# A linear-attention network on one core: every phi by two operations on ScalarE and one on VectorE, block sums moved behind the last keys, denominators at another pace

## The chip, the cores and the metric

The kernel runs on one core of one Trainium2 chip. The metric is the device time of one execution in microseconds (us). PE is TensorE's matmuls, PEld its weight loads, DVE is VectorE, ACT is ScalarE, POOL is GpSimd, SP the engine that issues most DMAs.

## The reference, cut to what matters

Four layers: linear attention (A), gated ReGLU (B), A, B, each on a layer norm and added back. x is 2048 x 1024, with 32 heads of 32.

```python
phi = lambda t: jnp.where(t > 0, t + 1, jnp.exp(t)) + 1e-6
pq, pk = phi(q), phi(k)
kv  = jnp.einsum("bhsd,bhse->bhde", pk, v)
z   = jnp.einsum("bhsd->bhd", pk)
num = jnp.einsum("bhqd,bhde->bhqe", pq, kv)
den = jnp.einsum("bhqd,bhd->bhq", pq, z)[..., None] + 1e-6
o = num / den          # then reshaped and multiplied by wo
```

Per attention there are 64 phis of 128 x 512 (32 of keys, 32 of queries).

## The kernel before

PE projects 128 x 512 blocks of keys and queries into PSUM banks (four "a" banks, and in the first three quarters two spare ones). A bank is free again when the last instruction of its phi has read it. In quarters 0 to 2 keys and queries alternate; the last quarter does its keys alone, then the products of keys and inputs over block sums, then its queries, between which stand four "folds" (kv times wo) with four copies each.

```python
def phi(self, ps, out, kind):
    nc = self.nc
    e = self.temp(dtype=BF16 if kind == "v" else F32)
    if kind == "v":
        nc.scalar.activation(out=e, in_=ps, func=ACT.Exp)                            # L375
    else:
        nc.scalar.activation(out=e, in_=ps, func=ACT.Relu, scale=-1.0)               # L377
        nc.scalar.activation(out=e, in_=e, func=ACT.Exp, scale=-1.0)                 # L378
        nc.scalar.activation(out=e, in_=e, func=ACT.Identity, bias=self.eps6[:, 0:1])# L379
    def join():
        if kind == "v":
            nc.vector.tensor_scalar(out=e, in0=e, scalar1=1.0, scalar2=1e-6,         # L383
                                    op0=ALU.min, op1=ALU.add)
        nc.vector.scalar_tensor_tensor(out=out, in0=ps, scalar=0.0, in1=e,           # L385
                                       op0=ALU.max, op1=ALU.add)
    # ... (in the first quarter join is put off by three steps)

# keys: always "v". Queries: "s", but "v" in the last quarter (of the second attention: half of it)
self.phi(project(f"q{c}", sc, j), pq[:, c * NW:(c + 1) * NW],
         "s" if sc < self.NQ - 1 or (l and j < 2) else "v")

# m_products, first attention: 64 block sums on VectorE (L485), four per step of PE
for n, (f, i) in enumerate(jobs):
    later.at(1 + n // 4, lambda f=f, i=i: f(i))
# ...
later.at(2 if l else 8, lambda: z_chain(0))

def z_chain(i):                     # denominators, one row of 128 after another
    z_mult(*divmod(i, QT))          # POOL multiplies (L595), DVE sums (L600) and inverts,
    if i < 10:                      # POOL scales the queries (L607)
        later.at(2, lambda: z_chain(i + 1))

def fold_wo(n):                     # ... 16 matmuls of 32x32 weights into four banks, then
    for i in range(R):              # R = 4
        dst = T[g // 4][:, g % 4, n2 * NW:(n2 + 1) * NW]
        nc.scalar.activation(out=dst, in_=ps[i], func=ACT.Copy)                      # L632
```

`later.at(n, f)` puts f into the program n ticks further on; a tick is one unit of PE's work. Vector instructions of the last quarter's queries are issued in program order; elsewhere a scheduler orders them when the kernel is built.

## Time and profile before

| | before |
|---|---|
| time | 1485.1 us, median of 3 (1484.46 to 1485.91) |
| profiled execution | span 1481.5 us, 1483.35 us as timed |
| busy PE, DVE, ACT, POOL | 1464.6, 880.9, 525.3, 285.2 us |
| matmuls | 6975, of which 6692 are of full size and 512 wide (not counting 11 at the start) |

### The profile page before, as it was taken

The page shows a single profiled execution, that of the slowest core. Times are in us where ns is not written, and L with a number is a line of the kernel's source. Part 1 is how long each engine was busy: PE and PEld are TensorE (multiplying, and loading weights), DVE is VectorE, ACT ScalarE, POOL GpSimd, SP SyncE. Part 2 cuts the span into 40 slices and gives each one's busy share as a digit, 9 for nine tenths or more (in the row PEclk, how much of TensorE's full clock was granted, in tenths as well). Part 3 has the DMA queues.
Part 4 walks back from the last instruction along what each step waited for, and adds up shares of the span by engine and source line. Part 5 has one row for each costly group of instructions (what it writes and reads, how often), then busy time and mean ns, then how long its engine had stood idle before and what let it go on. Part 6 is the DMA issues. An engine that isn't in the chain of part 4 may idle for free.

```text
span 1481.5 us, 18698 instructions
## 1 busy us (share of the span) xinstructions
PE 1464.6 (99%) x6975; PEld 664.5 (45%) x6975; DVE 880.9 (59%) x1551; ACT 525.3 (35%) x943; POOL 285.2 (19%) x190
## 2 busy tenths in 40 slices
PE   9989999999999999999999999999999999999999
PEld 4434444444444444444444444444444444444444
DVE  8996798666594543447368856874445434434632
ACT  6742413333340233341057525343333203333300
POOL 1442860111100011110023566401111000111000
PEclk9999999999999999999999999999999999999999
DMA  9930679565458963445943018994444698444461
GB/s 282 243 114 29 171 163 244 179 222 187 160 165 210 350 202 115 144 132 190 305 103 72 1 29 233 269 294 142 139 146 137 179 248 268 143 142 147 149 209 43
DMA packets 318363, 255.51 MB, mean 172 GB/s; under 512 B 105792, under 2 KB 291392, under 8 KB 317376
## 3 DMA queue, kind: packets, MB, share of 16 engines
q1 hardware_dynamic: 308304, 234.00, 54.5%
q10 hardware_dynamic: 9968, 20.32, 3.7%
q8 instruction: 54, 0.88, 0.3%
q14 instruction: 37, 0.30, 0.1%
HBM read 195.04 MB, written 34.60 MB: 155 GB/s over the span
## 4 chain that ended last, share of the span: by engine, by line
PE 88%; DVE 3%; POOL 1%; DMA 0%; issue 0%; SPq 0%; ACT 0%; DVEq 0%
PE yg L830 10%; PE yu L830 10%; PE dy L914 10%; PE ps L435 7%; PE ps L638 7%; PE dv L914 7%; PE dx L914 7%; PE xu L830 6%; PE xg L830 6%; PE vg L830 3%; PE vu L830 3%; PE zu L830 3%; PE zg L830 3%; PE my L517 2%; PE mx L517 2%; PE mv L517 1%
## 5 line engine op out<-in xcount | busy, mean ns | idle before, releaser
L830 PEld LDWEIGHTS <-w 128*128 128x128 f16 (+1 forms) x3136 | 306.5, 98 | 371.1 <-DVE w L764 0.9
L435 PE MATMUL ps<-w,xnT 128*128 128x512 bf16 x1024 | 224.5, 379 | 5.3 <-DVE slab L385 2.6
L868 POOL TENSOR_TENSOR h<-m5u,m5g 128x512 f16<-128x512 f32 x56 | 71.2, 1271 | 809.6 <-DVE m5u L864 787.8
L914 PEld LDWEIGHTS <-h 128*128 128x128 f16 x1120 | 109.6, 98 | 132.1
L861 DVE TENSOR_TENSOR zg<-yg,m5g 128x512 f32<-128x512 f32 x56 | 39.1, 699 | 197.5 <-PE yg L830 197.5
L435 PEld LDWEIGHTS <-xnT 128*128 128x128 bf16 x1024 | 99.4, 98 | 126.3 <-issue 8.8
L638 PE MATMUL ps<-T,pqT 128*128 128x512 bf16 x512 | 111.5, 379 | 4.5 <-DVE pq L385 4.4
L830 PE MATMUL xu<-xnT,w 128*128 128x512 f16 x448 | 115.3, 379 | 0.0
L830 PE MATMUL xg<-xnT,w 128*128 128x512 f16 x448 | 115.1, 379 | 0.0
L830 PE MATMUL yu<-s,w 128*128 128x512 f16 x448 | 115.0, 379 | 0.0
L830 PE MATMUL yg<-s,w 128*128 128x512 f16 x448 | 115.0, 379 | 0.0
L838 ACT ACTIVATE m5g<-m5g 128x512 f32<-128x512 f32 x56 | 35.2, 629 | 199.4 <-DVE m5g L864 199.4
L914 PE MATMUL dy<-w,h 128*128 128x512 f16 x448 | 98.0, 379 | 0.0
L914 PE MATMUL dx<-w,h 128*128 128x512 bf16 x448 | 97.3, 379 | 0.0
L595 POOL TENSOR_TENSOR kvc<-pq,kvc 128x1024 f32<-128x1024 bf16 x32 | 70.1, 2191 | 68.3 <-DVE den L600 48.9
L638 PEld LDWEIGHTS <-pqT 128*128 128x128 bf16 x512 | 50.0, 98 | 65.3 <-issue 5.7
L161 ACT ACTIVATE rstd<-mv,eps 128x1 f32<-128x1 f32 x64 | 18.1, 290 | 167.7 <-DVE mv L159 167.5
L154 DVE BATCH_NORM_STATS2 stats<-x 128x6 f32<-128x512 f32 (+1 forms) x120 | 76.5, 671 | 1.0 <-DMA x<-in_A_x_dram 0.8
L454 POOL TENSOR_TENSOR kvc<-kvc,slab 128x512 f32<-128x512 f32 x46 | 60.7, 1324 | 80.1 <-DVE slab L385 77.7
L841 DVE TENSOR_TENSOR h<-yu,r 128x512 f16<-128x512 f32 x56 | 38.7, 691 | 56.2 <-PE yu L830 56.2
L864 DVE TENSOR_TENSOR m5u<-yu,m5u 128x512 f32<-128x512 f32 x56 | 38.7, 691 | 54.6 <-PE yu L830 54.6
L914 PEld LDWEIGHTS <-e 128*128 128x128 f16 x448 | 43.8, 98 | 52.9
(126 smaller groups left out, 1985.2 us busy)
## 6 DMA issues: line engine op xcount, KB each, us to landing
w<-in_B_W_gate_dram SPq DMA_DIRECT2D x56, 512.0 KB, 6.0
w<-in_B_W_up_dram SPq DMA_DIRECT2D x56, 512.0 KB, 4.8
w<-td SPq DMA_DIRECT2D x32, 896.0 KB, 4.7
w<-in_B_W_down_dram SPq DMA_DIRECT2D x24, 896.0 KB, 5.6
w<-tg SPq DMA_DIRECT2D x42, 512.0 KB, 7.0
w<-tu SPq DMA_DIRECT2D x42, 512.0 KB, 6.1
w<-in_A_wqkv_dram SPq DMA_DIRECT2D x10, 1024.0 KB, 8.1
away<-x SPq DMA_DIRECT2D x16, 512.0 KB, 4.4
```

The lines of the kernel that those rows point to most:

```text
L154: self.nc.vector.bn_stats(out=stats[:, c, :], in_=src[:, c * fmax:(c + 1) * fmax])
L435: nc.tensor.matmul(by_row(ps), lhsT=self.xnT[l, l_q][:, kt, j * P:(j + 1) * P], rhs=w[:, kt, :].rearrange("p (b i d) -> p i b d", i=R, d=H ...
L454: nc.gpsimd.tensor_tensor(out=ksum[:, cols], in0=ksum[:, cols], in1=pk, op=ALU.add)
L517: nc.tensor.matmul(banks[j], lhsT=A(i)[:, j * P:(j + 1) * P], rhs=B(i), start=start and i == 0, stop=i == NS - 1, skip_group_check=True)
L595: nc.gpsimd.tensor_tensor(out=prod, in0=pq_of[sc, j], in1=zrow, op=ALU.mult)
L638: nc.tensor.matmul(ps, lhsT=pqT[sc][:, g, j * P:(j + 1) * P], rhs=T[g // 4][:, g % 4, n2 * NW:(n2 + 1) * NW], start=(g == 0), stop=(g == G ...
L830: nc.tensor.matmul(ps, lhsT=W[w][m][:, k, :], rhs=A[m][:, k, :], start=start and k == 0, stop=k == 3, skip_group_check=True)
L841: self.last_put = nc.vector.tensor_tensor(out=h[:, b, :], in0=ps, in1=R.pop(b), op=ALU.mult)
L861: nc.vector.tensor_tensor(out=Z[w], in0=Y[w], in1=V[w], op=ALU.add)
L864: nc.vector.tensor_tensor(out=V[w], in0=Y[w], in1=V[w], op=ALU.add)
L868: nc.gpsimd.tensor_tensor(out=h[:, 3, :], in0=V["u"], in1=V["g"], op=ALU.mult)
L914: nc.tensor.matmul(banks[j], lhsT=A(k)[:, j * P:(j + 1) * P], rhs=w[:, i, :], start=start and k == 0, stop=k == self.U - 1, skip_group_che ...
```

## The change

Its intent is to take VectorE work out of the way of PE. Each phi becomes exp(1e-6 - relu(-x)) on ACT in two operations and one VectorE instruction, max(x, 1e-6) plus that. The block sums of the first attention are issued behind the last phi of keys. The chain of denominators starts two steps earlier in the first attention and advances by 2 and 3 steps in turn instead of 2.

```diff
-    def phi(self, ps, out, kind):
+    def phi(self, ps, out):
...
-        e = self.temp(dtype=BF16 if kind == "v" else F32)
-        if kind == "v":
-            nc.scalar.activation(out=e, in_=ps, func=ACT.Exp)
-        else:
-            nc.scalar.activation(out=e, in_=ps, func=ACT.Relu, scale=-1.0)
-            nc.scalar.activation(out=e, in_=e, func=ACT.Exp, scale=-1.0)
-            nc.scalar.activation(out=e, in_=e, func=ACT.Identity, bias=self.eps6[:, 0:1])
+        e = self.temp()
+        nc.scalar.activation(out=e, in_=ps, func=ACT.Relu, scale=-1.0)
+        nc.scalar.activation(out=e, in_=e, func=ACT.Exp, scale=-1.0, bias=self.eps6[:, 0:1])
 
         def join():
-            if kind == "v":
-                nc.vector.tensor_scalar(out=e, in0=e, scalar1=1.0, scalar2=1e-6, op0=ALU.min,
-                                        op1=ALU.add)
-            nc.vector.scalar_tensor_tensor(out=out, in0=ps, scalar=0.0, in1=e,
-                                           op0=ALU.max, op1=ALU.add)
+            self.last_phi = nc.vector.scalar_tensor_tensor(out=out, in0=ps, scalar=1e-6, in1=e,
+                                                           op0=ALU.max, op1=ALU.add)
... (callers lose the kind)
+            last_k = self.last_phi
...
-                    later.at(1 + n // 4, lambda f=f, i=i: f(i))
+                    later.at(1 + n // 4, lambda f=f, i=i: self.behind(last_k, f, (i,)))
...
-            later.at(2 if l else 8, lambda: z_chain(0))
+            later.at(2 if l else 6, lambda: z_chain(0))
...
-                later.at(2, lambda: z_chain(i + 1))
+                later.at(2 + i % 2, lambda: z_chain(i + 1))
```

More of the change, by code (lines that the diff above doesn't have):

```diff
@@ L442, in k_unit @@
             pk = self.pk_home(l, t)
-            self.phi(project(f"k{c}", q, j, between), pk[:, c * NW:(c + 1) * NW], "v")
+            self.phi(project(f"k{c}", q, j, between), pk[:, c * NW:(c + 1) * NW])
             later.at(1 + (10 if self.phi_lag else 0), lambda: k_sum(t, slice(c * NW, (c + 1) * NW)))
@@ L582, in q_unit @@
             pq = pq_of[sc, j]
-            self.phi(project(f"q{c}", sc, j), pq[:, c * NW:(c + 1) * NW],
-                     "s" if sc < self.NQ - 1 or (l and j < 2) else "v")
+            self.phi(project(f"q{c}", sc, j), pq[:, c * NW:(c + 1) * NW])
             if c == H - 1 and lag is not None:
```

## The prediction

> **What bounds the kernel now.** I read four views: the page's busy times, who waited for whom with TensorE (PE) as the waiter, busy time by stretch, and the timeline of the worst stretch. The page first (busy us, share of the span, instructions):
>
> ```profile
> PE 1464.6 (99%) x6975; PEld 664.5 (45%) x6975; DVE 880.9 (59%) x1551; ACT 525.3 (35%) x943; POOL 285.2 (19%) x190
> ```
>
> PE is busy for 1464.6 of 1481.5 us, so all that a change on other engines can win is the remaining 16.9 us (1.1%), unless it removes matmuls, which this one doesn't. Is "busy" full speed? The chain of waits shows 112 matmuls of the down projection in 24.17 us, 0.216 us each; my count from the groups is 6692 matmuls 512 wide, 1445 us of the 1464.6. There is no hidden slack, and the granted clock is 1.0 in every stretch. Next, PE's waits (engine, line, releaser: us, times, longest):
>
> ```profile
> PE ps L638 <- DVE pq L385: 4.4, 2, 2.4
> PE ps L435 <- DVE slab L385: 2.6, 3, 1.2
> PE ps L435 <- DVE pq L385: 2.5, 3, 1.2
> PE mx L517 <- DVE slab L385: 1.8, 3, 0.9
> PE idle L246 <- DVE e L243: 1.3, 1, 1.3
> ```
>
> All but the start-up wait have one releaser: L385, the VectorE (DVE) instruction that ends a phi and gives its PSUM bank back. The four come to 11.3 us. Busy time by stretch says when (us, then PE, PEld, DVE, ACT, POOL busy, clock, DMA share, GB/s):
>
> ```profile
> 80.00:117.70 37.70, 31.42 (x141) 13.51 (x140) 36.95 (x61) 14.49 (x24) 18.45 (x13) 1.00 0.38 140
> ...
> 165.00:192.00 27.00, 21.93 (x167) 9.64 (x166) 24.72 (x32) 12.50 (x24) 19.74 (x10) 1.00 0.75 197
> 745.00:850.00 105.00, 105.00 (x488) 47.55 (x487) 87.97 (x157) 64.99 (x113) 39.49 (x31) 1.00 0.27 61
> 850.00:915.00 65.00, 64.91 (x389) 30.97 (x388) 41.18 (x71) 28.11 (x51) 49.65 (x25) 1.00 0.41 100
> ```
>
> PE loses 37.70 - 31.42 = 6.28 us where the first attention's last keys are made, and 27 - 21.93 = 5.07 us where its last queries are. Both times DVE is nearly full (98% and 92%). The second attention (the last two rows) loses 0.09 us. So only the first attention can pay.
>
> Why is DVE full there? The timeline of the last queries, DVE then POOL (GpSimd; in brackets, idle time before and its releaser):
>
> ```profile
> 170.13 1.83 DVE L383 TENSOR_SCALAR e<-e 128x512 bf16<-128x512 bf16 x1
> 172.06 0.69 DVE L385 SCALAR_TENSOR_TENSOR pq<-ps,e 128x512 bf16<-128x512 f32 x1
> 172.67 1.20 DVE L383 TENSOR_SCALAR e<-e 128x512 bf16<-128x512 bf16 x1
> 173.98 0.69 DVE L385 SCALAR_TENSOR_TENSOR pq<-ps,e 128x512 bf16<-128x512 f32 x1
> ```
>
> ```profile
> 169.69 2.12 POOL L595 TENSOR_TENSOR kvc<-pq,kvc 128x1024 f32<-128x1024 bf16 x1 [0.82 <-DVE den L600]
> 171.77 1.96 POOL L607 TENSOR_TENSOR pq<-pq,den 128x1024 bf16<-128x1024 bf16 x1
> ```
>
> L383, the min-and-add that the change deletes, takes 1.83 and 1.20 us and ends just when a POOL instruction ends (171.8, 173.8). Over the whole run:
>
> ```profile
> L383 DVE TENSOR_SCALAR e<-e x76: 241/282/1830, 14.1 to 915.7; 128x512 bf16<-128x512 bf16 x76
> ```
>
> Its median is 282 ns, its maximum 1830, its total 41.4 us (545 ns mean): it is cheap alone and dear beside POOL.
>
> **What the Trainium skill says.** "SBUF — State Buffer", section Who interferes with whom: VectorE and GpSimd share a port pair under an exclusive lock; tensor_scalar can enter a two-port mode and is then blocked for a whole GpSimd instruction; with two SBUF inputs it collides with GpSimd's reads; with at most one SBUF input outside those modes it does not. The trace agrees: L383 (one 16-bit SBUF source) reaches 1830 ns, the block sums L485 (two SBUF inputs) are 0.41 or 1.38 us, and L385 (PSUM and one SBUF input) stays at 0.69 beside the same POOL instructions. "ScalarE: Activation LUTs", section What ACT_TABLE_LOAD costs: a [128,1] pointer operand adds about 93 ns to an ACTIVATE, and ACTIVATEs back to back overlap by about as much. The trace agrees: 630 ns without (L378), 721 with (L379), yet both start 0.63 to 0.66 us apart.
>
> **The change, part by part.**
>
> 1. *VectorE.* 76 of 128 phis ran one ACT and two DVE operations ("v"), 52 three ACT and one DVE ("s"). All 76 L383 go: -41.4 us of DVE, 8.49 of it in 80-117.7, 11.54 in 165-192 (8 instructions), 13.6 in the second attention, where DVE was not in the way.
> 2. *ScalarE (ACT).* "v" goes from 588 ns to 592 + 721: 76 x 0.725 = +55 us. "s" loses an operation but its Exp gains the pointer: 52 x (592 + 721 - 592 - 630 - 721) = -32.8 us. Sum +22 us, 525 to about 548. While keys and queries alternate, the pitch per pair is 0.6 + 1.92 = 2.5 before and 2 x 1.27 = 2.5 after, against 3.46 us of PE for the two. Keys alone: 1.27 per 1.73. Neither binds.
> 3. *Block sums.* The 64 L485 of the first attention may no longer stand among the phis; the rebuilt order shows none ahead of the last key's phi. 18 of them, 11.57 us, leave the stretch 80-117.7. DVE there keeps about 37 - 8.5 - 11.6 = 17 us of work for 31 us of PE, even with all of L785, and PE's 6.28 us go. Are the sums now late? The third block product needs 16 of them, some 14 us after the last key phi; 16 x 0.41 is 6.6 us, 10 with POOL collisions. In the kernel before, DVE then idled 11.23 us. They fit.
> 4. *Last queries.* A period of two queries and a fold: DVE 1.83 + 0.69 + 1.20 + 0.69 + 1.74 (one denominator: 1.21 + 0.18 + 0.35) = 6.15 us, the period seen (170.13 to 176.32). PE needs 2 x 1.73 + 0.43 = 3.9. After: 1.38 + 1.74 = 3.1. PE binds again, and 5.07 us go.
> 5. *Given back.* ACT in that period: four fold copies at 0.48 pitch (1.93) and two phis (2.54) are 4.5 us against 3.9. Four periods leave ACT some 1.7 us behind, and a fold's banks wait for the copies of the fold before. The second attention before had almost this load (four "s" at 1.92, four "v") and lost nearly nothing, but one fold there stretched from 0.43 to 0.70. I choose 0.5 us for each attention: +1.0.
> 6. *Denominators' pace.* 2.5 ticks a row instead of 2 (4.3 against 3.5 us), where a POOL pair takes 4.0: DVE waits less at its head (L600 waited 15.3 us for POOL). PE's own order is unchanged line by line, and the output projections need the late rows long after. Nothing for PE in itself; worth 0.
>
> Sum: -6.28 - 5.07 + 1.0 = -10.3 us; 1485.1 becomes **1474.8**.
>
> **The rivals.** *ACT becomes the bound of the last queries*: for it, 4.5 against 3.9 and the longer chain to a bank's release (two ACT operations instead of one); against it, four banks and the second attention before. If the whole lag reached PE in both attentions: some +3.4 instead of +1.0, 1477. *A wait replaces the one removed*: the new DVE order puts all L785 (which need a load) ahead of the last keys, and without its backlog DVE could stand at one, or the late sums could hold the third product. For it: DVE is in order. Against: loads land in 7 us and were issued 8 or more us ahead. That would leave 3 to 6 us, 1478 to 1481. *The stall was elsewhere* (only L383 or only the order helps): the first stretch has 20 us of removable DVE work for 6.28, so either would do; the second depends on L383 alone. *Hidden anyway*: impossible for the 11.3 us, since PE itself stands idle.
>
> **Range and chances.** Best case is all 11.35 and a little more: 1473. A rival at half strength is 1479. Range 1472.0 to 1479.5. Faster by over 2% would take 29.7 us, more than PE's 16.9 of idle; slower by 2% would need a new stall larger than any seen. Hence 0.01, 0.97, 0.02.
>
> **What would show it.** PE's idle drops from 16.9 to about 6; DVE falls to some 835-840 us, ACT rises to about 548; L385 all but vanishes as releaser of PE; the block sums shorten from a mix of 0.41 and 1.38 towards 0.41; PE's waits, if any, name ACT (T or e) at the folds near 155-185. A releaser "DMA wd" or L485 would show the second rival. The prediction is wrong if PE's gaps at 80-117 or 165-192 stay although L383 is gone.

## The result, and the profile after

The changed kernel took 1471.41 us (median of 6, 1471.06 to 1472.55) against 1484.49 us for the kernel before (6 runs, 1483.82 to 1485.91): 13.08 us less. The ratio is 0.9913, with a 95% interval of 0.9900 to 0.9926. Ratios here are the mean time of one kernel's fast runs over that of the other's of the same rounds, so not quite the ratio of the medians quoted. The direction and the class (within 2%) are as predicted. The 1474.8 us and the lower end of the range, 1472.0, are not: the gain was 13 us, not 10.3.

The page of the changed kernel, first line of busy times:

```profile
PE 1460.8 (99%) x6937; PEld 664.4 (45%) x6975; DVE 839.7 (57%) x1475; ACT 551.5 (38%) x967; POOL 284.6 (19%) x190
```

VectorE lost 41.2 us (predicted 41.4) and ScalarE gained 26.2 (predicted 22). This trace lacks 38 records of matmuls, so its PE figure is not to be compared; the 6975 weight loads are complete. Who made PE wait, after:

```profile
PE idle L246 <- DVE e L243: 1.3, 1, 1.3
PE tp L286 <- DVE x L168: 1.1, 1, 1.1
PE vg L823 <- DVE s L796: 0.4, 1, 0.4
PE ps L428 <- ACT xnT L296: 0.2, 1, 0.2
```

The phi's last instruction (now L378) is gone from the list; what is left belongs to the start and, once, to the start of the second GLU. Busy time by stretch, for about the same two pieces of work (columns as in the prediction):

```profile
80.00:110.41 30.41, 30.36 (x142) 13.79 (x142) 19.79 (x31) 22.74 (x35) 16.25 (x13) 1.00 0.46 156
156.00:179.20 23.20, 23.03 (x173) 10.25 (x172) 14.45 (x25) 18.38 (x33) 17.28 (x10) 1.00 0.80 191
```

VectorE fell from 98% to 65% in the first and from 92% to 62% in the second, and PE is full in both. In the last queries VectorE now waits for ScalarE, not PE for VectorE (timeline of VectorE; in brackets its idle time and the releaser):

```profile
164.95 0.63 DVE L378 SCALAR_TENSOR_TENSOR pq<-ps,e 128x512 bf16<-128x512 f32 x1
167.53 0.69 DVE L378 SCALAR_TENSOR_TENSOR pq<-ps,e 128x512 bf16<-128x512 f32 x1 [1.95 <-ACT e L375]
168.14 1.21 DVE L593 TENSOR_REDUCE den<-kvc 128x32 f32<-128x1024 f32 x1
```

**A ruler that the idle view is not.** PE's order is the same in both kernels, so the k-th weight load of one trace can be set against the k-th of the other. From their start times I cut the run into stages. Here and below, "keys" is the time from the 309th weight load to the 501st (192 matmuls 512 wide: the end of the third quarter, the last keys, the start of the block products), and "last queries" from the 863rd to the 936th (from the third fold by the last query and the fourth fold into the output units: where the backlog of those queries reaches PE). "Folds 2" is the stage of the second attention's folds, "GLU 2" the start of the GLU behind it. All other stages agree within 0.3 us in all runs.

| stage, us | before | before, 2nd profile | after | after, 2nd profile |
|---|---|---|---|---|
| start, to the 309th load | 68.35 | 68.55 | 68.97 | 68.45 |
| keys | 49.31 | 50.49 | 41.44 | 41.44 |
| last queries | 17.06 | 17.08 | 11.90 | 11.90 |
| folds 2 | 25.24 | 25.26 | 25.30 | 25.28 |
| GLU 2 | 47.66 | 47.48 | 48.09 | 47.57 |
| span | 1481.54 | 1482.76 | 1469.65 | 1468.57 |

(The second profiles are runs e9 and e10 below.) 192 matmuls at 0.2158 us are 41.44 us: after the change the keys' stage has no stall at all, so the kernel before lost 7.87 us there, not the 6.28 that PE's idle time had shown. Of the last queries' stage 11.40 us can be had (runs e8 and e12 reach it), so it lost 5.66, not 5.07. Why the idle view shows less is seen on PE's timeline of the kernel before (start, length, count of matmuls; in brackets the idle time):

```profile
87.25 3.61 PE L435 MATMUL ps<-w,xnT 128*128 128x512 bf16 x16 [1.22 <-DVE pq L385]
91.56 8.83 PE L435 MATMUL ps<-w,xnT 128*128 128x512 bf16 x40 [0.69 <-DVE pq L385]
101.63 3.61 PE L435 MATMUL ps<-w,xnT 128*128 128x512 bf16 x16 [1.24 <-DVE slab L385]
105.50 1.89 PE L435 MATMUL ps<-w,xnT 128*128 128x512 bf16 x8 [0.26 <-DVE slab L385]
108.46 1.89 PE L435 MATMUL ps<-w,xnT 128*128 128x512 bf16 x8 [1.07 <-DVE slab L385]
```

Sixteen matmuls at 0.2158 us need 3.45 us, and they are shown as 3.61; eight need 1.73 and are shown as 1.89. Each record lasts 0.379 us while the next matmul may start 0.216 after it, so the last one before a pause covers 0.163 us of the pause, and a pause shorter than that is not shown at all. "Perfetto Trace Analysis", section Tensor Engine Instruction, says that the end of a PE record is an estimate from the instruction's size and a delay, a model and not a measurement. Whether a matmul is really at work for 0.379 us no run here shows, and the count does not need it: the starts alone say what was lost. In the kernel before, the keys' stage has 8 pauses: 6.28 + 8 x 0.163 = 7.6, near the 7.87. In its second profile 10 pauses: 7.41 + 10 x 0.163 = 9.04, and the weight loads say 9.05.

### The profile page after: what moved, and what is told of

Read it like the earlier page. It is cut to its first block, busy times and chain, and to the rows that moved or that the text cites. A ratio compares the mean times of both kernels' runs of the same rounds, so it can differ in the third digit from the quotient of the medians.

```text
span 1469.6 us, 18622 instructions
## 1 busy us (share of the span) xinstructions
PE 1460.8 (99%) x6937; PEld 664.4 (45%) x6975; DVE 839.7 (57%) x1475; ACT 551.5 (38%) x967; POOL 284.6 (19%) x190
## 4 chain that ended last, share of the span: by engine, by line
PE 94%; DVE 3%; ACT 1%; issue 1%; DMA 1%; DVEq 0%
PE ps L428 15%; PE yg L823 10%; PE yu L823 10%; PE dy L907 10%; PE dv L907 7%; PE dx L907 7%; PE xu L823 6%; PE xg L823 6%; PE ps L631 4%; PE vg L823 3%; PE zu L823 3%; PE zg L823 3%; PE vu L823 3%; PE my L511 3%; PE mv L511 2%; PE mx L511 2%
## 5 line engine op out<-in xcount | busy, mean ns | idle before, releaser
L375 ACT ACTIVATE e<-e,eps 128x512 f32<-128x512 f32 x128 | 92.4, 722 | 4.2
L374 ACT ACTIVATE e<-ps 128x512 f32<-128x512 f32 x128 | 75.9, 593 | 43.8 <-PE ps L428 42.6
L588 POOL TENSOR_TENSOR kvc<-pq,kvc 128x1024 f32<-128x1024 bf16 x32 | 73.7, 2302 | 62.4 <-DVE den L593 38.4
```

Source lines behind the costliest of these rows:

```text
L375: nc.scalar.activation(out=e, in_=e, func=ACT.Exp, scale=-1.0, bias=self.eps6[:, 0:1])
L588: nc.gpsimd.tensor_tensor(out=prod, in0=pq_of[sc, j], in1=zrow, op=ALU.mult)
```

## The experiments

Each expectation is quoted. Differences are to the median of the kernel before. Kernels are compared only within the same rounds.

| run | median, us | before | difference | ratio | keys | last queries | folds 2 |
|---|---|---|---|---|---|---|---|
| e1 new phi alone | 1471.77 | 1483.74 | -11.97 | 0.9917 | 43.00 | 11.90 | 25.28 |
| e2 order alone | 1476.56 | 1483.74 | -7.18 | 0.9950 | 41.44 | 18.63 | 25.24 |
| e3 pace alone | 1482.90 | 1483.74 | -0.84 | 0.9991 | 49.14 | 14.32 | 26.28 |
| e5 phi and order | 1470.63 | 1483.74 | -13.11 | 0.9907 | 41.44 | 11.90 | 25.28 |
| e8 no POOL work | 1478.77 | 1484.62 | -5.85 | 0.9957 | 49.13 | 11.40 | 25.25 |
| e11 order, phi of last queries | 1472.00 | 1484.62 | -12.62 | 0.9917 | 41.44 | 11.91 | 26.36 |
| e12 fold copy on DVE | 1470.16 | 1484.62 | -14.46 | 0.9902 | 41.44 | 11.40 | 24.76 |
| e10 the change again | 1470.87 | 1484.62 | -13.75 | 0.9909 | 41.44 | 11.90 | 25.28 |
| e13 as e5 | 1470.91 | 1484.88 | -13.97 | 0.9905 | 41.44 | 11.91 | 25.31 |
| e14 as e12 | 1470.03 | 1484.88 | -14.85 | 0.9897 | 41.44 | 11.40 | 24.76 |

The theory to test (A) was: two separate stalls, both made of VectorE work; the order of the sums or the new phi cures the first, the new phi alone the second. Rivals: the first stall needs the new order (B), the stall only moves (B2), the pace of the denominators does it (C). The rivals named D, L, N and F further down are told in the expectations of their runs.

**e1, the new phi alone.** The changed kernel, with these lines as before:

```diff
-                    later.at(1 + n // 4, lambda f=f, i=i: self.behind(last_k, f, (i,)))
+                    later.at(1 + n // 4, lambda f=f, i=i: f(i))
-            later.at(2 if l else 6, lambda: z_chain(0))
+            later.at(2 if l else 8, lambda: z_chain(0))
-                later.at(2 + i % 2, lambda: z_chain(i + 1))
+                later.at(2, lambda: z_chain(i + 1))
```

> The new phi alone, block sums and denominators as in the kernel before. Theory A (two stalls, both made of VectorE work; in the first stretch either the phi or the order is enough): 11 to 12.5 us faster than before, nearly all of the change. Rival B (the order of the block sums is needed for the first stretch): only 4 to 7 us faster, with PE still waiting for the phi's last instruction at 80 to 118 us.

It was 11.97 us faster, as A said, and B (4 to 7 us) falls. But the keys' stage is 43.00, so 1.56 us of stall are left there: the phi is not quite enough. VectorE's timeline of this run shows what stands between two phis of keys:

```profile
104.14 0.68 DVE L378 SCALAR_TENSOR_TENSOR slab<-ps,e 128x512 bf16<-128x512 f32 x1
104.74 0.68 DVE L778 TENSOR_TENSOR wd<-wd 128x1024 f16<-128x1024 bf16 x1
105.34 1.37 DVE L478 TENSOR_TENSOR x<-x,x 128x512 f16<-128x512 f16 x1
106.64 0.68 DVE L378 SCALAR_TENSOR_TENSOR slab<-ps,e 128x512 bf16<-128x512 f32 x1
```

A block sum (L478) of 1.37 us, where 0.41 is usual, and a weight sum make 2.50 us from phi to phi where PE delivers one each 1.73.

**e2, the order alone.** The kernel before, with the sums behind the last phi of keys:

```diff
-            nc.vector.scalar_tensor_tensor(out=out, in0=ps, scalar=0.0, in1=e,
+            self.last_phi = nc.vector.scalar_tensor_tensor(out=out, in0=ps, scalar=0.0, in1=e,
+            last_k = self.last_phi
-                    later.at(1 + n // 4, lambda f=f, i=i: f(i))
+                    later.at(1 + n // 4, lambda f=f, i=i: self.behind(last_k, f, (i,)))
```

> The old phi, only the block sums of the first attention behind the last phi of keys. Theory A: the first stretch is cured without the new phi, 5 to 8 us faster, the second stretch (165 to 192 us) stalls as before. Rival B2 (the stall only moves: the sums now hold up the third block product): under 3 us faster, with PE waiting for the sums.

It was 7.18 us faster. The keys' stage has no stall left (41.44), with all 76 min-and-adds in place, and the block products wait for nothing (their stage is 60.32 us before and here). So the order alone cures the first stretch, and B2 falls. The second stretch stalls as before; the run's longest wait of PE:

```profile
PE ps L639 <- DVE pq L385: 4.4, 2, 2.4
```

In this profile the stage is even longer than before (18.63 against 17.06), with the same waits. The weight loads after the longest one say why (start, length of one; in brackets the idle time of the load path):

```profile
184.76 0.15 PEld L639 LDWEIGHTS <-pqT 128*128 128x128 bf16 x1 [0.27 <-issue]
185.18 0.15 PEld L639 LDWEIGHTS <-pqT 128*128 128x128 bf16 x1 [0.28 <-issue]
185.61 0.15 PEld L639 LDWEIGHTS <-pqT 128*128 128x128 bf16 x1 [0.28 <-issue]
```

They come each 0.425 us for some 3 us, half the usual rate, and the granted clock is 0.51 in just that stretch (184.38 to 187.66), 0.97 over 155 to 186. The kernel before had the same wait without it. This profile is of the slowest of the five timed runs, which spread from 1475.60 to 1478.35 (those of e3 spread as far); how many of the others had the slow stretch is not known.

**e3, the pace alone.** The kernel before with the two changed lines of the denominators.

> The old phi and order, only the denominators at the new pace. Theory A: within 1.5 us of before, since VectorE stays the bound of the last queries. Rival C (the pace is what frees VectorE in the last queries): 3 us faster or more.

0.84 us faster, not distinguishable from nothing (interval 0.9978 to 1.0003); the profiled execution, the fastest of its five, was 2.04 us shorter than that of the kernel before. That is A's, but not by A's reasoning: the last queries' stage fell from 17.06 to 14.32, since fewer denominators stand between those phis, and 1.04 us were lost in the second attention's folds. Most of that loss (0.71 and 0.19 us) stands before two weight loads of the output units behind the fourth fold, and at the first of them PE waits for L385. Three of the min-and-adds of those queries last 1.24, 1.83 and 1.20 us there and overlap GpSimd's instructions, where the kernel before has at most 0.71. So a new pace alone also carries the old stall into the second attention.

**e5, phi and order without the pace.** The changed kernel with the last two edits of e1.

> The change without its third part, the pace. Theory A: as the whole change, 12 to 13 us faster than before, within 0.7 us of it. Rival C: 2 us or more short of the whole change, with VectorE's denominators waiting for GpSimd ahead of the last queries.

13.11 us faster, a hair above what was expected, and as much as the whole change (13.08). With the new phi in place the pace adds nothing; C falls.

**e8, without POOL's multiplications.** Its output is wrong, which doesn't matter for the time. Is a min-and-add slow because of POOL? The kernel before, with all VectorE instructions, and for the first twelve rows of the first attention without L595 and L607:

```diff
+            if l or sc > 2:
-            nc.gpsimd.tensor_tensor(out=prod, in0=pq_of[sc, j], in1=zrow, op=ALU.mult)
+                nc.gpsimd.tensor_tensor(out=prod, in0=pq_of[sc, j], in1=zrow, op=ALU.mult)
... (the scaling in z_scale likewise)
```

> WRONG RESULT on purpose: the kernel before without GpSimd's two multiplications for the first twelve rows of the first attention; every VectorE instruction, the 8 min-and-adds of the last queries among them, stays. Theory L (the min-and-adds are slow because GpSimd holds the shared port pair): they fall to 0.28 us each and the stage of the last queries from 17.1 to 12 to 12.6 us, the run 4.5 to 5.5 us faster than before. Rival N (it is the mere number of VectorE instructions): the stage stays within 1 us of 17.1.

5.85 us faster, and the last queries' stage is 11.40: no stall is left, more than L expected. The min-and-adds there (VectorE's timeline of this run):

```profile
170.84 0.23 DVE L383 TENSOR_SCALAR e<-e 128x512 bf16<-128x512 bf16 x1
171.17 0.69 DVE L385 SCALAR_TENSOR_TENSOR pq<-ps,e 128x512 bf16<-128x512 f32 x1
171.91 0.29 DVE L383 TENSOR_SCALAR e<-e 128x512 bf16<-128x512 bf16 x1
```

0.23 and 0.29 us where they took 1.83 and 1.20. This also takes away any wait of VectorE for POOL, but in the kernel before no such wait stood in this period: its 6.15 us were all busy time. So it is POOL's presence and not the number of VectorE instructions. The five traces with the old phi everywhere (before, e2, e3, e8, e9) agree: of their 76 min-and-adds, the 40 to 52 that overlap no POOL instruction last 0.295 us at most, and every one over 0.4 us overlaps one. "SBUF — State Buffer", section Who interferes with whom, names the way: tensor_scalar can enter a mode that takes the port pair which VectorE shares with GpSimd, and then one of the two blocks the other for a whole instruction. The traces fit it, but no run separates this lock from another effect of POOL.

Not tested is whether POOL makes the first stall too. In the stretch 80 to 117.7 of the kernel before, 13 min-and-adds took 8.49 us and 18 block sums 11.57; at their usual 0.28 and 0.41 they would take 3.7 and 7.4 (an estimate). These 9 us are as much as the stall, but e8 left POOL's work of that stretch in place, and its keys' stage (49.13) stayed.

**e11, the least that should do.** e2, with the new phi for the last queries only (the eight of the first attention, four of the second), the old one elsewhere.

> The old phi everywhere but in the last queries (8 of the first attention, 4 of the second), with the block sums behind the last phi of keys, old pace. Theory A (each stall needs one part only): as the whole change, 12 to 13.3 us faster than before. Rival D (the new phi of the keys pays too): 1 us or more short of it.

12.62 us faster, as A said, but also 1.13 us behind the changed kernel (e10, 1470.87), as D said. The stages decide: both stalls are cured (41.44, 11.91), so beside the new order the new phi of the keys pays nothing, and D falls. It is the second attention's folds that lost 1.1 us (26.36). PE's timeline there:

```profile
895.45 0.66 PE L630 MATMUL fold<-w,kvc 32*32 32x512 bf16 x16
...
899.60 1.31 PE L630 MATMUL fold<-w,kvc 32*32 32x512 bf16 x16
...
904.40 0.94 PE L630 MATMUL fold<-w,kvc 32*32 32x512 bf16 x16
```

A fold that waits for nothing lasts 0.43. In this kernel the folds' stage has four old phis of 1.92 us of ACT and four new ones of 1.27, more than either kernel: 12.8 us, against 4 x 1.92 + 4 x 0.6 = 10.1 before and 8 x 1.27 = 10.2 after. That would be the given-back term of the prediction, larger because the load is: against e5 the whole 1.08 us stand inside two folds. That it is ACT's load here was not tested by a run of its own.

**e12, one fold copy of four on VectorE.** e5, with

```diff
-                nc.scalar.activation(out=dst, in_=ps[i], func=ACT.Copy)
+                if i == R - 1:
+                    nc.vector.tensor_copy(out=dst, in_=ps[i])
+                else:
+                    nc.scalar.activation(out=dst, in_=ps[i], func=ACT.Copy)
```

> New phi and new order, old pace, and one of the four copies of each fold on VectorE instead of ScalarE. Theory F (what is given back, 0.5 us at the fourth fold, is ScalarE's lag): the fold after the first output unit no longer waits, 0.3 to 0.8 us faster than new phi and order without it, so 13.3 to 14 us faster than before. Rival (VectorE has no room beside the denominators): equal or slower, PE waiting for VectorE.

In the changed kernel PE's fourth fold of the first attention lasts twice its usual time:

```profile
172.83 1.89 PE L631 MATMUL ps<-T,pqT 128*128 128x512 bf16 x7
174.65 0.94 PE L619 MATMUL fold<-w,kvc 32*32 32x512 bf16 x16
175.52 0.82 PE L631 MATMUL ps<-T,pqT 128*128 128x512 bf16 x3
```

In e12 it is

```profile
174.81 0.43 PE L619 MATMUL fold<-w,kvc 32*32 32x512 bf16 x16
```

and the stage falls from 11.90 to 11.40, that of the second folds from 25.28 to 24.76. So the 0.5 us were ACT's lag at the folds, as F said. The median was 14.46 us faster than before, above the expected 13.3 to 14, by which the call's slower kernel before (1484.62) has its part.

**e10, the changed kernel again; e9, the kernel before again.** No edit.

> The changed kernel once more. If the first 12 us of a run vary from execution to execution (arrival of the first loads), the start up to the first projections differs from the 5.70 us of its first profile by up to 0.7 us and the rest of the run by less than 0.3 us; 12.3 to 13.3 us faster than before. If the new pace costs 0.4 us at the start of the second GLU, that wait is there again.

> The kernel before, profiled once more. If the stalls are fixed by the program and the first 12 us by the arrival of loads, the keys' stage is 49.1 to 49.5 us and the last queries' 16.9 to 17.2 us again, and the whole span differs from 1481.5 us by up to 1.3 us, nearly all of it ahead of the keys' stage.

e10 was 13.75 us faster than before, more than expected. The wait for loads at its start was shorter (5.02 us against 5.70 between the first weight load and the first transpose's), and the 0.4 us at the second GLU's start were mostly not there again (47.57), so that was chance and not the pace; my "rest within 0.3 us" missed by that stage. e9, a single execution (1484.54 us, state unknown, as for any single run), missed its expectation usefully: its keys' stage took 50.49 us instead of 49.1 to 49.5. Its start was only 0.2 us slower. Its waits of PE have five, not three, of

```profile
PE ps L435 <- DVE pq L385: 3.7, 5, 0.9
```

So the stall in the kernel before is not a fixed size; four profiles with that stall (before, e3, e8, e9) show 49.13 to 50.49. What shifts it is not settled. The profile on which the prediction was built, timed at 1483.35 us, was a favourable one. Over the two pairs of profiles the difference is 11.89 (before and after) and 14.19 us (e9 and e10), 13.04 in the mean, next to 13.08 as timed.

**e13 and e14, e5 and e12 once more.** No new edit.

> New phi and order, old pace, once more, beside the next kernel in one call: 12.5 to 13.3 us faster than before.

> The same with one fold copy in four on VectorE. Theory F: 0.5 to 1.0 us faster than the kernel beside it (0.5 us in the last queries of the first attention, 0.5 us in the folds of the second); the stages show it whatever the medians do.

13.97 us faster (1470.32 to 1471.14) and 14.85 us faster (1469.25 to 1470.20): e13 above its expectation of 12.5 to 13.3, against a kernel before that had 1484.88 this time. The two don't overlap, 0.9 us apart. The best version is therefore new phi, new order, old pace, and one fold copy of four on VectorE; it gives a correct result, at a ratio of 0.9897 to before.

## Why the prediction was right or wrong, point by point

| term | predicted, us | measured in the traces, us |
|---|---|---|
| keys' stall removed | -6.28 | -7.87, in the second pair -9.05 |
| last queries' stall removed | -5.07 | -5.66 |
| given back to ACT | +1.0 | +0.50 in the first attention, under 0.1 in the second |
| start, second GLU | 0 | +1.05 in the first pair, -0.01 in the second |
| sum | -10.3 | -11.9 and -14.2; as timed -13.08 |

- *Where the time is: right.* Only the first attention paid, in the two stretches named, and its releaser vanished.
- *The size of what can be won: wrong, and this is the step that failed.* "PE loses 37.70 - 31.42 = 6.28 us" and "27 - 21.93 = 5.07" took PE's idle time for its loss. The weight loads show 7.87 and 5.66: 2.2 us more. Of this, 1.8 us are the 0.163 us that each of the 11 pauses shown hides under the record of the last matmul; the rest lies in pauses too short to be shown. "There is no hidden slack" was said of the rate while PE runs, where it holds; nothing was said of the edges of the pauses. For the same reason "Best case is all 11.35 and a little more: 1473" was no best case.
- *A single profile as the base: a second, smaller error of the same step.* The profile read had the smaller stall; another execution lost 1.2 us more in the keys' stage. The range had no room for that on the fast side. Apart from the gain, 0.6 us of the miss is the base: 1485.1 was the median of three runs, that of six is 1484.49.
- *Part 1, VectorE -41.4, and part 2, ScalarE +22: right in kind and nearly in size* (-41.2, +26.2). No stage shows a cost of the 4 us more of ScalarE.
- *Part 3, the sums fit: right.* The block products' stage kept its 60.32 to 60.34 us; no block sum held PE there. That "either would do" in the first stretch was half right: the order alone cures it wholly (e2), the phi alone leaves 1.56 of 7.87 us (e1).
- *Part 4, the last queries: right in mechanism.* The doubled min-and-adds were the stall, and POOL was what doubled them (e8).
- *Part 5, given back: right in mechanism, twice too large.* e12 shows that ACT's lag at the folds was the cause. The waits view named no releaser for it; it showed as a fold of 0.94 instead of 0.43 us. (The prediction's "four periods leave ACT some 1.7 us behind" is the sum of three: 4.5 less 3.9 is 0.6 a period.)
- *Part 6, the pace: right that it is worth nothing here* (e5 against the change), but "Nothing for PE in itself" does not hold with the old phi, where it took 2.74 us off the last queries' stage (e3).
- *The rivals.* ACT came as a bound at the fourth fold of each attention only, and cost 0.5 to 0.6 us more than before in all, instead of that rival's 3.4; no wait took the place of the ones removed; no DMA shows as a releaser of PE in either stretch ("loads land in 7 us" was loose: the five of wd took 3.9 to 10.0, median 5.2).

## What to carry to other kernels

Where PE is 99% busy, what a change can win is the sum of PE's pauses, and that is to be measured from start to start against the steady pitch: in this case by adding 0.163 us (0.379 less 0.216) per pause to the idle time shown, or best by comparing the same weight load's start in two traces. An instruction that is cheap alone and runs beside GpSimd is to be judged by its durations where PE waits, not by its median over the run; here 0.28 us became 1.83, and removing eight of them was worth 5.2 us. And before giving a range, profile the same kernel twice: here one stall differed by 1.2 us between two profiles of one kernel.

## What the Trainium skill lacked or had wrong

- "Perfetto Trace Analysis", section Tensor Engine Instruction: it says that a PE record's end is estimated, but not what this does to idle time. The runs show 0.163 us of each pause hidden: 6.28 us shown for 7.87 lost, 7.41 for 9.05.
- "TensorE: Matmul & The Clock Gate", section Back-to-back issue gap: it gives about 131 ns a matmul for a sustained stream of weight loads and matmuls 512 wide, and about 216 for an isolated one. Here 192 such pairs in a row took 41.44 us, 215.8 ns each, in every run without a stall there: the figure for the isolated one is that of the stream.
- The same page, section What's actually happening: it puts the fall to half rate after an idle window of about 3.4 us. In e2 weight loads came each 0.425 us for some 3 us, at a granted clock of 0.51, after a wait shown as 2.38 us; in the profile of the kernel before the same wait had no such effect. What decides between the two no run here shows.
